# An mLSTM and mixture-of-experts kernel: SyncE's transfers in the recurrent part wait for the sixth one before them

## The chip, the cores and the metric

One core of a Trainium2 chip runs the whole program in one launch. The metric is the device time of an execution in microseconds, as the median of several executions.

## What is computed

The first part is an mLSTM layer on 4 batches x 8 heads, 768 steps, head size 40. Each step of the reference updates a matrix state and gives one row of the output:

```python
m_new = np.maximum(f_gate[:, :, t] + m, i_gate[:, :, t])
f_stab, i_stab = np.exp(f_gate[:, :, t] + m - m_new), np.exp(i_gate[:, :, t] - m_new)
C = f_stab[:, :, None, None] * C + i_stab[:, :, None, None] * np.einsum('bhd,bhe->bhde', vt, kt)
n = f_stab[:, :, None] * n + i_stab[:, :, None] * kt
h_tilde = np.einsum('bhde,bhe->bhd', C, qt)
denom = np.maximum(np.abs(np.einsum('bhd,bhd->bh', n, qt)[:, :, None]), 1.0)
y[:, :, t] = 1.0 / (1.0 + np.exp(-o_gate[:, :, t])) * h_tilde / denom
```

The second part takes the 3072 rows of that output (320 wide). It sends each to the one of 8 experts whose embedding is closest, and that expert gives `relu(x @ w1) @ w2` (1024 hidden units), times the router's share.

## The kernel before

The mLSTM is computed in tiles of 128 steps of one batch: 24 tiles, numbered `n`, in the order of the steps with the four batches inside. One turn of the Python loop `for n in range(NS)` is called a step below. The program is written out in full, and every engine's order of work is the order in which the source issues it (a manual schedule); waits are derived from the buffers.

In a step TensorE adds the tile's keys and values to the state (`stage_add`, L610), computes the scores of the next tile (`stage_scores`, L571), turns an earlier tile for the router (L716 to L718), sums the output (`stage_y`, L653 and L664) and scores it against the embeddings (L730). GpSimd scales the values of tile `n + 2` (`stage_uv`, L556) and multiplies the output of tile `n - 1` by its gate (`stage_gate`, L700). VectorE masks the scores (L580), divides (L696) and does the router's small operations. ScalarE copies.

All bulk transfers of this part are issued by SyncE, one after the other, in this order in each step `n`:

- `load_dims(n + 5)`: two loads into `kq_s` (L541), each of 40 rows of 4096 bytes (160 KB). There are NQ = 6 buffers, so the buffer of tile `n - 1` must be free.
- `load_rows(n + 5)`: one load into `kv_s` (L537), 128 rows of 2592 bytes (324 KB), also 6 buffers.
- `stage_sig(n + 3)`: one load of the output gate into `sig` (L550), 160 KB.
- `stage_store(n - 1)`: one store of the gated rows to `x_d` in DRAM (L704), 160 KB, which waits for L700.
- From step 9 on, in the steps of `W_AT`, one piece of an expert's weights into `raw` (L173 to L179), 256 to 512 KB.

Before the loop, the loads of tiles 0 to 4 and of the first gates are issued in the same way. After step 23 come the experts: first hidden products of the earliest tokens (L374), sums (L406), then the six other experts with weights that arrive one expert ahead. Transfers of that part are issued by SyncE (weights, and stores `x_d<-halves` followed by transposes at L1470) and by GpSimd (gathers and scatters).

Nothing in the source before limits how many of SyncE's transfers are under way.

Of the kernel before, what the change touches and what calls it, by code (L numbers as in the profile page):

```python
# [26 lines left out]
DM = H * D  # L27
P = 128
L = 64
# [4 lines left out]
NQ = 6  # L34
# [24 lines left out]
EMB_AT = (2, 3, 4)  # L59
ROOTS = {6: (0, 4), 10: (4, 8), 15: (8, 13), 18: (13, 16), 22: (16, 20)}  # L60
FILLS = (9, 3, 3)
NK = 2
NJ = NW // NK
RANGE = 60.0
# [5 lines left out]
def tile_mlstm_moe(  # L70
# [22 lines left out]
    V, G, A, T, SY = nc.vector, nc.gpsimd, nc.scalar, nc.tensor, nc.sync  # L93
# [65 lines left out]
    wrev_p = cp.tile([P, E], F32, name="wrev_p")  # L159


    def load_expert(e, at=None):
        raws, ws = {}, {}
        w1_, w2_ = (w[e] if at is None else w[ds(at, 1)].rearrange("o p f -> (o p) f") for w in (w1, w2))

        def load(i, part=None):
            def go():
                if not part:
                    raws[i] = wp.tile([P, F], F32, name=f"raw_{e}_{i}", tag="raw", bufs=7)
                raw = raws[i]  # L170
                w = slice(0, F) if part is None else slice(part * (F // 2), (part + 1) * (F // 2))
                if i < 2:
                    SY.dma_start(raw[:, w], w1_[i * P : (i + 1) * P, w])  # L173
                elif i == 2:
                    SY.dma_start(raw[0:L, w], w1_[2 * P : DM, w])
                    SY.dma_start(raw[L:P, w], w1_[2 * P : DM, w])
                else:
                    c = slice(2 * (i - 3), 2 * (i - 3) + 2)
                    SY.dma_start(  # L179
                        raw[:, 0 : 2 * DM].rearrange("p (c d) -> p c d", c=2),  # L180
                        w2_.rearrange("(c p) d -> p c d", p=P)[:, c],
                    )

            return go

        def piece(i, half, eng=None, on_act=True):
            def go():
                if i < 3:
                    c = slice(half * 512, half * 512 + 512)
                    h, lo, src = ws["w1h"][:, i, c], ws["w1l"][:, i, c], raws[i][:, c]  # L190
                else:
                    c = 2 * (i - 3) + half
                    h, lo, src = ws["w2h"][:, c], ws["w2l"][:, c], raws[i][:, half * DM : (half + 1) * DM]
                if on_act:
                    A.copy(h, src)  # L195
                else:
                    V.tensor_copy(h, src)
                (eng or V).tensor_tensor(lo, src, h.bitcast(F32), ALU.subtract)  # L198

            return go  # L200

        def tiles(pool, k):
            for t in "hl":
                shape = [P, 3, F] if k == 1 else [P, FC, DM]
                ws[f"w{k}{t}"] = pool.tile(shape, F32R, name=f"w{k}{t}_{e}", tag=f"w{k}{t}")

        return dict(ws=ws, tiles=tiles, load=load, piece=piece)
# [270 lines left out]
    with ExitStack() as actx:  # L478
# [20 lines left out]
        en = wp.tile([E, DM], F32, name="en", tag="raw", bufs=7)  # L499
# [13 lines left out]
        kv_s = [ap1.tile([P, KV], F32, name=f"kv_s{i}") for i in range(NQ)]  # L513
# [10 lines left out]
        st, sigs, xs_, grp = {}, {}, {}, {}  # L524
# [9 lines left out]
            return (t[:, a : a + 2 * NP * d].rearrange("p (c a d) -> p c a d", c=2, a=NP) for a, d in ((0, D), (m, D1)))  # L534

        def load_rows(n):
            SY.dma_start(kv_s[n % NQ], kv[n])  # L537

        def load_dims(n):
            for r in range(2):  # L540
                SY.dma_start(  # L541
                    kq_s[n % NQ][r * L : r * L + D, r : r + 2].rearrange("d w a t -> d (w a t)"),
                    kq[n, r].rearrange("d w a t -> d (w a t)"),
                )

        def stage_sig(n):
            j, b = divmod(n, B)
            if b == 0:
                sigs[j] = tp.tile([P, B, DM], F32, name=f"sig_{j}", tag="sig", bufs=2)
            SY.dma_start(sigs[j][:, b], og[:, n])  # L550

        def stage_uv(n, engs=None):
            j, b = divmod(n, B)
# [147 lines left out]

        def stage_store(n):
            j, b = divmod(n, B)
            SY.dma_start(xrows(j)[:, b, 0:DM], xs_[j][:, b])  # L704


        def stage_sq(n):
# [30 lines left out]
        def xrows(j):  # L738
            return x_d[0:NT].rearrange("(j b p) d -> j p b d", b=B, p=P)[j]
# [276 lines left out]
        V.memset(naught, 0.0)  # L1016
        fill(FILLS[0])
        V.memset(flat(kq_s[1]), 0.0)
# [13 lines left out]
        for n in range(3, 5):  # L1032
            load_dims(n)
            load_rows(n)
            if n == 3:
                SY.dma_start(en, emb)
        stage_sig(2)
        A.dma_start(taub, tau.partition_broadcast(P))

# [160 lines left out]
        w_loads, exps = [], {}  # L1200
# [9 lines left out]
        for n in range(NS):  # L1210
            last = n == NS - 1
            if n + 5 < NS:
                load_dims(n + 5)
                load_rows(n + 5)
            if n + 3 < NS:
                stage_sig(n + 3)
            if n == W_AT[0]:
                for k in range(NE):
                    exps[k] = load_expert(
                        k, nc.values_load(first[0:1, k : k + 1], engines=[ET.SP], min_val=0, max_val=E - 1)  # L1220
                    )
                exps[0]["tiles"](wp, 1)
                w_loads = [exps[0]["load"](i, part) for part in range(2) for i in range(3)]
                w_loads += [exps[0]["load"](i) for i in range(3, 7)] + [exps[1]["load"](i) for i in range(2)]
            stage_add(n, 0)
            stage_mid(n)
            for k in of(n - 1, 1, NEXT_AT):
                stage_keep(k)
            if n == 1:
                gates_exp()  # L1230
                A.activation(maxc.bitcast(F32), half, AF.Sigmoid)
            if n == 2:
                stage_sigmoid(1)
            if not last:
                stage_scores(n + 1)
            if n + 2 < NS and n not in (1, 2):
                stage_uv(n + 2)
            if n == NS - 4:
                gates_early[2]()
            if n:  # L1240
                for k in range(3):
                    stage_den(n - 1, k)
                stage_x(n - 1)
                for k in of(n, 1):
                    stage_gate(k, G if n < NS - 2 else V)
            if n == 1:
                stage_uv(n + 2)
            if n == NS - 3:
                for i in range(NE * HT):
                    gather_a(*divmod(i, HT))  # L1250
            if not last:
                stage_weigh(n + 1)
            for k in of(n, 1, NEXT_AT):
                stage_next(k)
            route(n)
            tick(9)
            if n == 0:
                gates_floor()
            if n == 1:
                gates_spread()  # L1260
            if n == 2:
                gates_turn()
                stage_uv(n + 2)
            if n == EMB_AT[2]:
                embeddings(2)
            if last:
                x_tile(xa[0], xs_a[:, 0], 0, pS, "ps")
            for k in of(n, 2):
                stage_xt(k)
            if last:  # L1270
                x_tile(xa[0], xs_a[:, 0], 1, pM, "pm")
            stage_y(n)
            if n < NS - B:
                stage_add(n, 1)
            if n != 1:
                stage_sigmoid(n)
            if n == 0:
                A.activation(maxc.bitcast(F32), half, AF.Exp)
            for k in of(n, 1):
                stage_store(k)  # L1280
            for k in of(n, 2):
                stage_sq(k)
            if n in EMB_AT[:2]:
                embeddings(EMB_AT.index(n))
            if n == 3:
                numbers()
            if n in (5, 6):
                G.memset(xs_a[:, n - 5], 0.0)
            if n == 5:
                more_numbers()  # L1290
            for k in of(n, 3, (EMB_AT[2],)):
                stage_logits(k)
            for _ in range(W_AT.count(n)):
                if w_loads:
                    w_loads.pop(0)()
            if n in W1_AT:
                exps[0]["piece"](*PIECES1[W1_AT.index(n)], G)()
            if n in ROOTS:
                gates_root(*ROOTS[n])
# [51 lines left out]
        n, g = NS - 1, len(GROUPS) - 1  # L1351
# [171 lines left out]
    for i in range(NE * HT):  # L1523
        e, a = divmod(i, HT)
# [14 lines left out]
    for e in range(NE, E):  # L1539
        j = e - NE  # L1540
        ws, x, w = exps[e]["ws"], xp, slice(0, CAPS[j])
        xps, turns, gt = [], [], gts[j]
        if e + 1 < E:
# [7 lines left out]
            n = CAPS[j + 1]  # L1551
# [30 lines left out]
    with tc.If(over > 0):  # L1582
        with ExitStack() as octx:
# [15 lines left out]
            with tc.For_i(0, steps, 1) as t:  # L1599
# [12 lines left out]
                kv = op.tile([NH, D, D], F32, name="kv")  # L1612
# [19 lines left out]
            with tc.For_i(0, again, 1):  # L1632
                V.tensor_copy(expert, num)
                for n in range(NS):
                    j, b = divmod(n, B)
# [46 lines left out]
            with tc.For_i(0, E, 1) as k:  # L1682
# [10 lines left out]
                with tc.For_i(0, NS, 1) as t:  # L1693
                    xo = op.tile([P, XW], F32, name="xo")
                    go = xo[:, DM:XC]
# [9 lines left out]
                    for c in range(3):  # L1705
                        w = min(P, DM - c * P)
# [3 lines left out]
                    for f in range(FC):  # L1710
                        ph = pv.tile([P, 512], F32, name=f"ovh_{f}", tag="ovh")
                        for c in range(3):
                            w = min(P, DM - c * P)
# [71 lines left out]
```

## Time and profile before

| what | value |
|---|---|
| time, median of 3 executions | 324.54 us (321.11 to 327.33) |
| profiled execution, its own time | 324.12 us |
| its span, first to last instruction | 322.3 us |
| TensorE busy | 299.6 us (93%) |
| VectorE, ScalarE, GpSimd busy | 217.6, 167.2, 169.6 us |
| SyncE's data queue, share of 16 DMA engines' time | 57.5% |

The profiled execution took 1.8 us more than its span. The mLSTM's steps fill the span from about 10 to 112 us, the experts the rest. A page of the profile cuts the span in 40 slices of 8.06 us; its first 14 digits belong to the mLSTM. "Issue" in a list of waits or in the chain is time in which an engine waited for nothing that the profile shows.

### The profile page before, as it was taken

Reading aid. Unit: us, or ns where it says so; the run is one execution under the profiler, and the core shown is the slowest. Engines: PE = TensorE matmul, PEld = TensorE weight load, DVE = VectorE, ACT = ScalarE, POOL = GpSimd, SP = SyncE. Lnnn points to the kernel's source line nnn. Section 1 sums busy time; section 2 is a strip of 40 time slices with the busy share of each in tenths; the row PEclk is TensorE's granted clock in tenths of the full one; section 3 lists DMA queues with packets and bytes.
Section 4 is the critical chain, followed back from the end, with each engine's and each line's share of the span. In section 5 each row is a group of like instructions: output and inputs, shape, how many; then the busy total and the mean of one; then the engine's idle time right before and its main releaser. Section 6 shows DMA issues by size and latency. Waiting matters only on the chain.

```text
span 322.3 us, 9598 instructions
## 1 busy us (share of the span) xinstructions
PE 299.6 (93%) x3637; PEld 284.5 (88%) x3637; DVE 217.6 (68%) x607; ACT 167.2 (52%) x429; POOL 169.6 (53%) x205
## 2 busy tenths in 40 slices
PE   6899996998777999999879999999999999999992
PEld 2889996997676999899879999999999999999992
DVE  7777896858894579865544876666756696586630
ACT  6676774775643586253232754546337266265310
POOL 8788865787867178150752850640650751632112
PEclk9799999999989799999979999999999999999998
DMA  5898998999986682130479968968948929837001
GB/s 136 261 303 295 287 278 266 263 272 290 284 238 174 183 222 71 13 86 2 125 243 181 301 189 210 320 195 235 247 150 228 290 94 288 235 103 219 21 22 39
DMA packets 48089, 63.31 MB, mean 196 GB/s; under 512 B 21146, under 2 KB 37990, under 8 KB 48034
## 3 DMA queue, kind: packets, MB, share of 16 engines
q1 hardware_dynamic: 45218, 54.16, 57.5%
q0 software_dynamic: 2560, 8.35, 8.9%
q8 instruction: 31, 0.51, 0.7%
q14 instruction: 24, 0.20, 0.2%
q10 hardware_dynamic: 256, 0.10, 0.1%
HBM read 47.51 MB, written 11.93 MB: 184 GB/s over the span
## 4 chain that ended last, share of the span: by engine, by line
PE 77%; DVE 11%; ACT 4%; issue 3%; DMA 3%; another core or an unknown queue 0%; POOL 0%; POOLq 0%; DVEq 0%; ACTq 0%; SPq 0%
PE ph L374 27%; PE po L406 17%; PE s L571 7%; PE y L653 4%; PE po_b L406 4%; PE y L664 3%; PE c L610 3%; PE po L391 3%; DMA kq_s<-in_kq 2%; PE pm L730 2%; PE po_a L406 2%; PE px L716 1%; ACT w2h L195 1%; DMA x_d<-x 1%; DVE w_s L580 1%
## 5 line engine op out<-in xcount | busy, mean ns | idle before, releaser
L425 POOL DMA_INDIRECT out<-ob,ids x20 | 22.2, 1112 | 75.4 <-DVE ob L422 64.6
L376 ACT ACTIVATE hh<-ph 128x448 fp32r<-128x448 f32 (+2 forms) x48 | 23.6, 492 | 42.8 <-PE ph L374 23.7
L406 PE MATMUL po<-w2h,hl 128*128 128x320 f32 x128 | 39.6, 309 | 0.0
L406 PE MATMUL po<-w2h,hh 128*128 128x320 f32 x128 | 39.5, 309 | 0.0
L406 PE MATMUL po<-w2l,hh 128*128 128x320 f32 x128 | 39.5, 309 | 0.0
L556 POOL TENSOR_TENSOR uv<-kv_s,u_t 64x328 f32<-64x328 f32 x47 | 35.0, 744 | 5.8 <-DMA kv_s<-in_kv 3.1
L571 PE MATMUL s<-kq_s 128*64 128x64 f32 x768 | 30.5, 230 | 4.6 <-issue 3.8
L571 PEld LDWEIGHTS s<-kq_s 128*64 128x64 f32 x768 | 27.8, 144 | 6.1 <-issue 4.5
L379 DVE SCALAR_TENSOR_TENSOR hl<-ph,hh 128x384 fp32r<-128x384 f32 (+1 forms) x48 | 24.4, 509 | 12.4 <-ACT hh L376 11.6
L374 PE MATMUL ph<-xh,w1h 128*128 128x448 f32 (+2 forms) x96 | 32.0, 336 | 0.0
L374 PE MATMUL ph<-xh,w1l 128*128 128x448 f32 (+2 forms) x96 | 32.0, 336 | 0.0
L195 ACT CAST w1h<-raw 128x512 fp32r<-128x512 f32 x48 | 28.9, 613 | 2.2 <-DMA raw<-in_w 2.2
L195 ACT CAST w2h<-raw 128x320 fp32r<-128x320 f32 x62 | 24.6, 457 | 7.0 <-DMA raw<-in_w 5.2
L422 DVE TENSOR_SCALAR ob<-po,gt 128x320 f32<-128x320 f32 x16 | 8.8, 550 | 27.9 <-PE po L406 19.8
L198 DVE TENSOR_TENSOR w2l<-raw,w2h 128x320 fp32r<-128x320 f32 x58 | 26.5, 504 | 1.1 <-ACT w2h L195 0.5
L297 POOL DMA_INDIRECT xs<-x_d,ids x20 | 22.9, 1143 | 6.2 <-issue 5.8
L198 DVE TENSOR_TENSOR w1l<-raw,w1h 128x512 fp32r<-128x512 f32 x36 | 24.7, 694 | 1.5 <-ACT w1h L195 1.5
L653 PE MATMUL y<-uv,w_s 128*64 128x82 f32 x384 | 24.8, 249 | 0.0
L374 PE MATMUL ph<-xl,w1h 128*128 128x448 f32 (+2 forms) x96 | 24.5, 336 | 0.0
L626 ACT COPY c_mid<-c 40x164 f32<-40x164 f32 x48 | 14.0, 292 | 19.7 <-PE c L610 15.6
L406 PEld LDWEIGHTS po<-w2l,hh 128*128 128x128 f32 x128 | 24.0, 188 | 0.0
L406 PEld LDWEIGHTS po<-w2h,hh 128*128 128x128 f32 x128 | 24.0, 188 | 0.0
(313 smaller groups left out, 912.8 us busy)
## 6 DMA issues: line engine op xcount, KB each, us to landing
raw<-in_w SPq DMA_DIRECT2D x32, 320.0 KB
kv_s<-in_kv SPq DMA_DIRECT2D x24, 324.0 KB
kq_s<-in_kq SPq DMA_DIRECT2D x48, 160.0 KB
raw<-in_w SPq DMA_DIRECT2D x14, 512.0 KB
raw<-in_w SPq DMA_DIRECT2D x18, 256.0 KB
sig<-in_og SPq DMA_DIRECT2D x24, 160.0 KB
x_d<-x SPq DMA_DIRECT2D x24, 160.0 KB
x_d<-halves SPq DMA_DIRECT2D x4, 576.0 KB
```

The costliest lines, as they stand in the source:

```text
L195: A.copy(h, src)
L198: (eng or V).tensor_tensor(lo, src, h.bitcast(F32), ALU.subtract)
L297: G.indirect_dma_start(out=xs[0 : c.shape[0], a], out_offset=None, in_=x_d[0:rows], in_offset=bass.IndirectOffsetOnAxis(ap=c, axis=0), bou ...
L374: T.matmul(ph, lt, rh, start=i == 0, stop=i == len(ops) - 1)
L376: A.activation(hh, ph, AF.Relu)
L379: V.scalar_tensor_tensor(hl[:, 0:m], ph[:, 0:m], 0.0, hh[:, 0:m].bitcast(F32), ALU.max, ALU.subtract)
L406: T.matmul(po[0 : ts_.stop - ts_.start, 0:DM], lt[f][:, ts_], rh[:, f], start=k == 0, stop=k == len(ops) - 1)
L425: store = G.indirect_dma_start(out=out, out_offset=bass.IndirectOffsetOnAxis(ap=slots, axis=0), in_=ob, in_offset=None, bounds_check=NT - ...
L556: eng.tensor_tensor(uv[n % NB][rows, :, :, r], list(rows_of(n))[1][rows], u_t[rows, j, b].unsqueeze(3).broadcast_to([L, 2, NP, D1]), ALU.mult,
L571: T.matmul(s[r * L : r * L + L, c, p], k_of(n, odd)[:, a, cs], q_of(n)[:, a, cs], start=True, stop=True,)
L626: A.copy(dst, src)
L653: T.matmul(yh[c][:, g, :, odd], w_s[n % NB][:, c, 2 * g + odd], uv[n % NB][:, c, 2 * g + odd], start=g + odd == 0, stop=n < B and c == 0, ...
```

## The change

Each of the transfers named above goes through a new function `paced`, which keeps a list in the order of issue. From the seventh on, a transfer gets a dependency on the one six places ahead of it: SyncE issues it only when that one has landed. Not in the list are the first gates (L507), the row of zeros (L1192), the gates' columns (L472), the weights that are issued after the loop, and everything of the experts' part.

```diff
+UNDER_WAY = 6
+    under_way = []
+    def paced(dma):
+        under_way.append(dma.ins)
+        if len(under_way) > UNDER_WAY:
+            tc.add_manual_dep(
+                dma.ins,
+                under_way[-1 - UNDER_WAY].name,
+                mybir.DependencyInfo(mybir.DependencyClass.Sync, mybir.DependencyReason.DATA),
+                reason="few transfers under way",
+            )
...
-            def go():
+            def go(send=SY.dma_start):
...
-                    SY.dma_start(raw[:, w], w1_[i * P : (i + 1) * P, w])
+                    send(raw[:, w], w1_[i * P : (i + 1) * P, w])
...
-            SY.dma_start(kv_s[n % NQ], kv[n])
+            paced(SY.dma_start(kv_s[n % NQ], kv[n]))
...
-                SY.dma_start(
+                paced(SY.dma_start(
                     kq_s[n % NQ][r * L : r * L + D, r : r + 2].rearrange("d w a t -> d (w a t)"),
...
-            SY.dma_start(sigs[j][:, b], og[:, n])
+            paced(SY.dma_start(sigs[j][:, b], og[:, n]))
...
-            SY.dma_start(xrows(j)[:, b, 0:DM], xs_[j][:, b])
+            paced(SY.dma_start(xrows(j)[:, b, 0:DM], xs_[j][:, b]))
...
-                SY.dma_start(en, emb)
+                paced(SY.dma_start(en, emb))
...
-                    w_loads.pop(0)()
+                    w_loads.pop(0)(lambda *a: paced(SY.dma_start(*a)))
```

## Rows read from the trace of the kernel before

**Rows 1.** The page: busy tenths in 40 slices, and a DMA queue (packets, MB, share).

```profile
PE   6899996998777999999879999999999999999992
DMA  5898998999986682130479968968948929837001
...
q8 instruction: 31, 0.51, 0.7%
```

**Rows 2.** Timeline of SyncE's queue, 1 to 16 us: start, duration, line, transfer.

```profile
1.94 0.68 SPq L541 DMA_DIRECT2D kq_s<-in_kq  x2
2.66 0.36 SPq L537 DMA_DIRECT2D kv_s<-in_kv  x1
3.70 0.66 SPq L541 DMA_DIRECT2D kq_s<-in_kq  x2
4.40 0.40 SPq L537 DMA_DIRECT2D kv_s<-in_kv  x1
4.84 0.50 SPq L550 DMA_DIRECT2D sig<-in_og  x1
6.35 0.69 SPq L541 DMA_DIRECT2D kq_s<-in_kq  x2
7.52 0.35 SPq L537 DMA_DIRECT2D kv_s<-in_kv  x1
```

**Rows 3.** Timeline of TensorE, 5 to 40 us; in brackets idle time and what ended it.

```profile
7.64 1.15 PE L571 MATMUL s<-kq_s 128*64 128x64 f32 x32 [0.56 <-DMA kq_s<-in_kq]
...
10.54 1.97 PE L571 MATMUL s<-kq_s 128*64 128x64 f32 x32 [0.15 <-DMA kq_s<-in_kq]
```

**Rows 4.** The chain that ended last, in order of time: start, duration, work.

```profile
36.45 0.93 PE s L571 x32
...
40.07 0.93 PE s L571 x32
...
43.35 0.31 PE c L610 x8
```

**Rows 5.** Timeline of GpSimd, 5 to 52 us.

```profile
14.55 1.54 POOL L556 TENSOR_TENSOR uv<-kv_s,u_t 64x328 f32<-64x328 f32 x2 [0.68 <-DMA kv_s<-in_kv]
...
36.49 1.58 POOL L556 TENSOR_TENSOR uv<-kv_s,u_t 64x328 f32<-64x328 f32 x2
```

**Rows 6.** Stretches: busy us of PE, PEld, DVE, ACT, POOL; clock, DMA share, GB/s.

```profile
20.00:24.00 4.00, 4.00 (x95) 3.76 (x94) 2.75 (x13) 3.15 (x12) 3.20 (x5) 1.00 0.91 311
44.00:48.00 4.00, 4.00 (x111) 3.71 (x107) 3.67 (x14) 2.84 (x11) 2.46 (x5) 1.00 0.92 281
52.00:56.00 4.00, 1.57 (x31) 1.15 (x28) 2.24 (x7) 1.16 (x4) 1.36 (x2) 1.00 0.79 246
84.00:88.00 4.00, 2.18 (x62) 1.98 (x57) 3.44 (x11) 1.28 (x6) 3.85 (x5) 1.00 0.90 277
...
94.50:98.30 3.80, 3.80 (x74) 3.77 (x70) 2.47 (x10) 1.99 (x8) 3.13 (x4) 0.55 0.64 142
```

**Rows 7.** SyncE's waits, whole span: us in total, times, longest.

```profile
SPq L1470 <- DMA x_d<-halves: 11.0, 6, 2.6
...
SPq L541 <- DMA kq_s<-in_kq: 5.2, 10, 0.9
SPq L550 <- DMA kq_s<-in_kq: 5.2, 10, 0.9
```

**Rows 8.** Timeline of TensorE at its two longest "issue" waits.

```profile
55.00 0.33 PE L718 MATMUL px<-ident,x 128*128 128x128 f32 x1 [2.43 <-issue]
...
87.13 0.69 PE L571 MATMUL s<-kq_s 128*64 128x64 f32 x17 [1.82 <-issue]
```

**Rows 9.** Timeline of SyncE's queue, 47 to 89 us.

```profile
47.12 0.70 SPq L541 DMA_DIRECT2D kq_s<-in_kq  x2
...
54.64 0.35 SPq L550 DMA_DIRECT2D sig<-in_og  x1
...
81.67 0.35 SPq L537 DMA_DIRECT2D kv_s<-in_kv  x1
...
88.50 0.53 SPq L175 DMA_DIRECT2D raw<-in_w  x1
```

More of the change, by code (lines that the diff above doesn't have):

```diff
@@ L172, in go @@
                 if i < 2:
-                    SY.dma_start(raw[:, w], w1_[i * P : (i + 1) * P, w])
+                    send(raw[:, w], w1_[i * P : (i + 1) * P, w])
                 elif i == 2:
-                    SY.dma_start(raw[0:L, w], w1_[2 * P : DM, w])
-                    SY.dma_start(raw[L:P, w], w1_[2 * P : DM, w])
+                    send(raw[0:L, w], w1_[2 * P : DM, w])
+                    send(raw[L:P, w], w1_[2 * P : DM, w])
                 else:
                     c = slice(2 * (i - 3), 2 * (i - 3) + 2)
-                    SY.dma_start(
+                    send(
                         raw[:, 0 : 2 * DM].rearrange("p (c d) -> p c d", c=2),
@@ L536, in load_rows @@
         def load_rows(n):
-            SY.dma_start(kv_s[n % NQ], kv[n])
+            paced(SY.dma_start(kv_s[n % NQ], kv[n]))
         def load_dims(n):
             for r in range(2):
-                SY.dma_start(
+                paced(SY.dma_start(
                     kq_s[n % NQ][r * L : r * L + D, r : r + 2].rearrange("d w a t -> d (w a t)"),
                     kq[n, r].rearrange("d w a t -> d (w a t)"),
-                )
+                ))
         def stage_sig(n):
```

## The prediction

> **What bounds the kernel now.** I read the page first, for where TensorE and the DMA engines are both full; then the timeline of SyncE's queue, because the change touches nothing else; then the timelines of TensorE and GpSimd for who starts at the moment a transfer lands; and the stretches for the price of a step.
>
> TensorE is nearly full for most of the span [rows 1]. In the mLSTM from 20 to 52 us it is full: 4.00 of 4.00 us in the stretches at 20 and 44 us [rows 6], and the scores of one tile follow those of the last after 40.07 - 36.45 = 3.62 us [rows 4]. In the same stretches the 16 DMA engines are busy 0.91 and 0.92 of the time [rows 6]. So this part runs on two resources of about the same length; TensorE ends last.
>
> Before about 17 us it is the transfers that end last. TensorE's scores of tiles 0 and 1 start at 7.64 and 10.54 us, each on a `kq_s` transfer [rows 3], and GpSimd's scaling of tile 2 at 14.55 us on a `kv_s` transfer [rows 5].
>
> SyncE already holds transfers back. It waits ten times for a `kq_s` transfer before it issues another `kq_s`, and ten times before a `sig` [rows 7], though those transfers share no buffer. How far back that reaches can be counted in the list of issues [rows 2]: the load of tile 2's `kv_s` goes out at 7.52 us, next to TensorE's start at 7.64 us on tile 0's second `kq_s` transfer [rows 3]. Between that transfer (issued at about 2.3 us) and the `kv_s` load stand `kv_s` 0, two `kq_s` 1, `kv_s` 1, `sig` 0 and two `kq_s` 2, which are seven; so the one eight places ahead was awaited. **So the kernel has at most eight under way, and the change makes it six**, not six in place of any number.
>
> **Does a transfer land later?** A step issues 5 transfers (two `kq_s`, `kv_s`, `sig`, the store) in 3.62 us, one in 0.72 us. With eight under way, each may take 8 x 0.72 = 5.8 us from issue to landing. By the count above it is 5.3 us at the start (2.3 to 7.6). With six, each may take 6 x 0.72 = 4.3 us. The question is what of the 5.8 us is the transfer's own and what is queue. A lone transfer shows the first: SyncE waits for the landing of the stores `x_d<-halves` 11.0 / 6 = 1.8 us after their issue [rows 7], with an issue of about 0.4 us (`kv_s` at 4.40 us, rows 2) 2.2 us in all. So 3.6 us are queue, and a DMA share of 0.9 [rows 6] says the same: the engines have work waiting. With six, a new transfer finds five ahead of it, 5 x 0.72 = 3.6 us of work, and needs at most 2.2 us to take its place behind them. The engines don't run dry; cover 1.4 us. Transfers go out later by up to 1.5 us and land as before. Cost: 0.
>
> Behind a waiting transfer on SyncE stand the next loads, the gate loads and the stores. Who waits for them: TensorE for `kq_s`, GpSimd for `kv_s`. If the cover of 1.4 us is gone, a second one stands behind it in the steps: GpSimd scales tile 9 at 36.49 us, is done at 38.07 us [rows 5], and TensorE adds the product at 43.35 us [rows 4], 5.3 us later. At the start there is none: tile 2's scaling ends at 16.09 us [rows 5], about when TensorE needs it. What the start could lose is bounded by 0 and, if the latency of 5.3 us stayed with six under way, by 2.0 us: nine transfers stand ahead of `kv_s` 2, and 5.3 / 6 = 0.88 us for each in place of 5.3 / 8 = 0.66 makes 2.0 us. I take 0, for the queue argument holds there too.
>
> Stores land in DRAM for gathers much later. Pieces of weights stand among paced transfers in steps 9 to 23; each waits for the sixth before it in place of the eighth, 1.5 us later, and lands behind the same queue: 0. The wait itself costs no engine but SyncE, which computes nothing. The experts' part is not touched: 0.
>
> **What may be gained.** TensorE stops twice for nothing that the profile shows, 2.43 us before 55.00 us and 1.82 us before 87.13 us [rows 8]. These are the stretches in which its busy time falls to 1.57 and 2.18 of 4 us [rows 6]. A queue of its own brings 31 blocks of instructions, 0.51 MB [rows 1], and runs on the same 16 engines. The two stops fall where data is slowest: the second `kq_s` transfer of the row at 47.12 us has `sig` at 54.64 us as its eighth follower, 7.2 us later, and `kv_s` at 81.67 us has the weights at 88.50 us, 6.8 us later [rows 9], against the usual 5.8. If a block of instructions waits as data does, the queue ahead of it shrinks by 5.8 - 4.3 = 1.5 us, and so does each stop: at most 2.9 us. If it doesn't, 0. Nothing in the trace separates the two; I take the middle, 1.45 us. What is gained at 55 us reaches the end: TensorE is full after it.
>
> The Trainium skill, DMA: Bandwidth & Descriptors, section on queues, rings and completion order, says that a DMA engine takes turns between its queues, packet by packet. By that rule a block of instructions would never wait behind SyncE's whole queue, the stops would stay, and the time would be that of the second rival. No row here shows the order inside an engine.
>
> **The sum.** The profiled execution took 324.12 us, 322.3 of span and 1.8 around it. Landing later 0, gain 1.45: 322.7. The median of the runs stands 0.4 above the profiled one (324.54), so 323.1 us.
>
> **The rivals.**
>
> *Slower: the latency doesn't shrink.* If what I call queue is the transfer's own time under load, six under way give 6 in 5.3 us in place of 8: a step's five take 4.4 us, 0.8 more than TensorE's 3.62. Tiles 7 to 23 are loaded in steps 2 to 18, some 16 steps: 12.8 us, less the cover of 5.3 us, gives +7.5 us, 332 us. It decides from 0.33 us more in a step (5.3 / 16), that is from a landing time of 6 x (3.95 / 5) = 4.7 us with six under way. Against it: lone transfers at 2.2 us and a DMA share of 0.9. For it: TensorE and the DMA are so close to each other that little must go wrong.
>
> *No difference.* Transfers go out later and land as before, and the stops stay (or lie elsewhere): 324.5 us. For it: the stops may come from the moment of the request and not from its queue.
>
> *Faster: the stops go altogether.* 2.43 + 1.82 = 4.25 us, and with the second the slow clock may go: in the stretch at 94.5 us, 6.5 us behind the half-busy one at 84, the granted clock is 0.55 over 3.80 us (mostly the lower level, 1.2 GHz), 1.7 us lost [rows 6]. 324.5 - 5.95 = 318.6 us.
>
> **How the numbers follow.** Chances: the forecast 0.56, no difference 0.22, slower 0.12, faster 0.10. A measurement of this kernel can tell about 2%, 6.5 us: its three times lie 6.2 us apart. The forecast's own range is 321 to 326 (gain of 0 to 2.9, and half of the spread of the runs). To hold 8 in 10, the range reaches to 318.5, the faster rival, and to 329.5, a slower rival at two thirds of its price. Faster by over 2% (under 318) needs more than the faster rival's sum, 0.06; slower (over 331) is most of the slower rival, 0.09; within it 0.85.
>
> **What would show it.** In SyncE's timeline the first `sig` load moves from 4.84 to about 6.3 us and tile 2's first `kq_s` from 6.35 to about 7.5 us; counted six places back, a landing takes some 4.3 us. TensorE still starts scores at 7.6 and 10.5 us, and GpSimd tile 2 at about 14.6 us. The steps stay at 3.62 us with a DMA share of 0.9. The stops near 55 and 87 us shorten by about 1.5 us or not at all. Steps over 3.95 us, a DMA share near 0.75, and TensorE waiting for `kq_s` or for L556 after 20 us would make the slower rival right; times of scores before 17 us that are later by 1 us or more would show the start's cover gone.

## The result and the profile after

The changed kernel takes 328.75 us (median of 20 executions, 324.63 to 335.54), the kernel before beside it 324.25 us (20 executions, 320.44 to 327.33). The ratio of the two is 1.0112, 95% interval 1.0071 to 1.0153: **1.1% slower**, where 0.4% faster was forecast. The ratio is smaller than that of the medians because it leaves out disturbed executions, as do all ratios below. The profiled execution took 328.64 us, 326.9 of it span, against 324.12 and 322.3.

First what came as forecast. SyncE's timeline of the changed kernel (start, duration, line; lines behind the new function stand 14 higher than before, and the pieces of weights are now issued at L1309), which answers to [rows 2]:

```profile
2.66 0.37 SPq L551 DMA_DIRECT2D kv_s<-in_kv  x1
...
6.27 0.35 SPq L564 DMA_DIRECT2D sig<-in_og  x1
7.58 1.14 SPq L555 DMA_DIRECT2D kq_s<-in_kq  x2
9.49 0.35 SPq L551 DMA_DIRECT2D kv_s<-in_kv  x1
```

`sig` has moved from 4.84 to 6.27 us and tile 2's `kq_s` from 6.35 to 7.58 (forecast: 6.3 and 7.5). The first users start when they did, TensorE's scores of tiles 0 and 1 [rows 3] and GpSimd's scaling of tile 2 [rows 5]:

```profile
7.66 1.72 PE L585 MATMUL s<-kq_s 128*64 128x64 f32 x32 [0.58 <-DMA kq_s<-in_kq]
...
10.60 1.51 PE L585 MATMUL s<-kq_s 128*64 128x64 f32 x32 [0.23 <-DMA kq_s<-in_kq]
```

```profile
14.54 1.56 POOL L570 TENSOR_TENSOR uv<-kv_s,u_t 64x328 f32<-64x328 f32 x2 [0.61 <-DMA kv_s<-in_kv]
```

Then what didn't. The same stretches as in [rows 6], with two more (columns as there: busy time of five engines, granted clock, DMA share, GB/s):

```profile
20.00:24.00 4.00, 4.00 (x98) 3.76 (x95) 2.82 (x13) 2.75 (x10) 2.76 (x5) 1.00 0.88 287
44.00:48.00 4.00, 3.89 (x105) 3.51 (x103) 3.70 (x12) 2.58 (x9) 2.79 (x4) 1.00 0.89 261
52.00:56.00 4.00, 3.79 (x107) 3.49 (x104) 3.90 (x10) 2.15 (x7) 3.85 (x5) 1.00 0.82 258
57.50:60.50 3.00, 0.09 (x3) 0.07 (x4) 2.23 (x7) 1.20 (x4) 0.54 (x1) 0.78 0.89 246
59.20:66.00 6.80, 5.57 (x84) 5.45 (x85) 1.82 (x8) 4.15 (x13) 5.73 (x7) 0.50 0.96 292
84.00:88.00 4.00, 4.00 (x114) 3.76 (x109) 2.98 (x8) 3.86 (x13) 2.35 (x3) 1.00 0.95 282
```

The stretches at 52 and 84 us, which TensorE's two stops had half emptied, are full: 3.79 and 4.00 us in place of 1.57 and 2.18. The stops of [rows 8] are gone altogether. But from 20 to 48 us the transfers move less: 311 GB/s at 20 us has become 287, 281 at 44 us 261. And a new hole stands at 57.5 us, where TensorE works 0.09 of 3.00 us, with the lower clock (0.50) for 6.80 us behind it.

The chain that ended last says what this is. By engine, over the whole span, before and then after:

```profile
PE 77%; DVE 11%; ACT 4%; issue 3%; DMA 3%; another core or an unknown queue 0%; POOL 0%; POOLq 0%; DVEq 0%; ACTq 0%; SPq 0%
```

```profile
PE 61%; DMA 23%; DVE 5%; POOL 3%; issue 3%; ACT 1%; another core or an unknown queue 1%; SPq 1%; POOLq 0%; DVEq 0%
```

Transfers make up 23% of the chain in place of 3%. Its pieces in the first 56 us (start, duration, what):

```profile
1.94 4.27 DMA kq_s<-in_kq
6.27 5.37 DMA sig<-in_og
11.65 5.10 DMA kq_s<-in_kq
16.77 4.11 DMA sig<-in_og
20.89 5.26 DMA kq_s<-in_kq
26.22 4.48 DMA kv_s<-in_kv
...
40.97 4.63 DMA kv_s<-in_kv
45.61 4.89 DMA sig<-in_og
...
55.75 3.49 DMA raw<-in_w
```

The first six pieces hang together, each beginning where the last one landed: 1.94 + 4.27 = 6.21, and the sixth follower goes out at 6.27. This is the change's own dependency, end to end, up to 30.70 us. After that the chain runs through GpSimd, TensorE and ScalarE as well, and only the piece at 45.61 us begins at a landing again. The trace's semaphore updates tell when every transfer has landed: 88 of the 111 paced transfers up to `kv_s` 23 go out within 0.15 us of the landing of the one six places ahead, the others later, for other reasons.

The lag of this list decides when the first piece of weights (`raw`) goes out, at 55.75 us. SyncE's lines around it, the kernel before and then the changed one:

```profile
49.02 0.35 SPq L550 DMA_DIRECT2D sig<-in_og  x1
...
51.46 0.36 SPq L173 DMA_DIRECT2D raw<-in_w  x1
```

```profile
49.46 0.35 SPq L551 DMA_DIRECT2D kv_s<-in_kv  x1
...
53.31 0.35 SPq L564 DMA_DIRECT2D sig<-in_og  x1
...
55.75 0.36 SPq L1309 DMA_DIRECT2D raw<-in_w  x1
```

The gate load `sig` at 53.31 us waits for the `kv_s` load six places ahead, which was issued at 49.46 and landed at 53.25 us. From this gate load to the piece 2.44 us pass in both kernels.

That piece ends the hole at 57.5 us. ScalarE's cast of it, of the kernel before and then of the changed one, with TensorE's stop:

```profile
57.18 0.62 ACT L195 CAST w1h<-raw 128x512 fp32r<-128x512 f32 x1 [0.52 <-DMA raw<-in_w]
```

```profile
59.26 0.62 ACT L209 CAST w1h<-raw 128x512 fp32r<-128x512 f32 x1 [4.62 <-DMA raw<-in_w]
59.79 0.59 ACT L640 COPY c_mid<-c 40x164 f32<-40x164 f32 x2
...
60.43 0.40 PE L678 MATMUL y<-c_mid,kq_s 128*64 128x82 f32 x1 [2.91 <-ACT c_mid L640]
```

The piece goes out 4.29 us later. ScalarE stands 4.62 us for it, and behind the cast in ScalarE's order stands the copy `c_mid`, which TensorE's sum needs: 2.91 us. The lower clock from 59.2 us begins within that stop. The cast starts 2.08 us later than before, for the late piece landed sooner after its issue (3.49 us). By this count the other 0.8 us of the stop would have been left with the piece on time: without its first stop TensorE reaches this place about 2 us sooner.

Where the time went, by the starts of TensorE's scores (us):

| what starts | before | after | difference |
|---|---|---|---|
| scores of tile 12 | 51.10 | 51.45 | +0.4 |
| tile 13 (first stop of before lies ahead of it) | 57.35 | 55.33 | -2.0 |
| tile 14 | 60.95 | 63.55 | +2.6 |
| tile 16 | 68.29 | 72.13 | +3.8 |
| tile 21 (second stop of before lies ahead of it) | 90.31 | 92.49 | +2.2 |
| tile 23 | 100.62 | 103.70 | +3.1 |
| first hidden product of the experts | 111.52 | 114.60 | +3.1 |
| end of span | 322.3 | 326.9 | +4.6 |

The first stop gone gives 2.4 us. From tile 13 to 16, 5.9 us are lost: the stop of 2.91, and the lower clock over 5.57 us of TensorE's work, half of which (2.8) is its price at a granted clock of 0.50. The second stop gone gives 1.7 back. The last 1.5 us are lost in the experts' part, where the lower clock lasts 6.8 us from 165.0 in place of 3.4 us from 162.9; the change paces no transfer there, and what lengthens the low clock isn't shown.

### The profile page after: what moved, and what is told of

Same layout as the page of the kernel before. It is cut to its first block, busy times and chain, and to the rows that moved or that the text cites. A ratio compares the mean times of both kernels' runs of the same rounds, so it can differ in the third digit from the quotient of the medians.

```text
span 326.9 us, 9598 instructions
## 1 busy us (share of the span) xinstructions
PE 302.7 (93%) x3637; PEld 287.3 (88%) x3637; DVE 218.6 (67%) x607; ACT 167.3 (51%) x429; POOL 170.0 (52%) x205
## 4 chain that ended last, share of the span: by engine, by line
PE 61%; DMA 23%; DVE 5%; POOL 3%; issue 3%; ACT 1%; another core or an unknown queue 1%; SPq 1%; POOLq 0%; DVEq 0%
PE ph L388 27%; PE po L420 17%; DMA kq_s<-in_kq 9%; DMA sig<-in_og 6%; PE po_b L420 4%; PE po L405 3%; DMA kv_s<-in_kv 3%; DMA raw<-in_w 2%; PE s L585 2%; DMA xs_a<-x_d,ids_a 2%; PE y L667 2%; PE y L678 2%; PE c L624 1%; POOL uv L570 1%
## 5 line engine op out<-in xcount | busy, mean ns | idle before, releaser
L585 PE MATMUL s<-kq_s 128*64 128x64 f32 x768 | 29.2, 231 | 1.0 <-DMA kq_s<-in_kq 1.0
L212 DVE TENSOR_TENSOR w2l<-raw,w2h 128x320 fp32r<-128x320 f32 x58 | 27.2, 515 | 0.6
L678 PE MATMUL y<-c_mid,kq_s 128*64 128x82 f32 x192 | 23.1, 246 | 3.0 <-ACT c_mid L640 2.9
L311 POOL DMA_INDIRECT xs<-x_d,ids x20 | 21.5, 1073 | 6.2 <-issue 5.8
```

The source lines that it names most:

```text
L311: G.indirect_dma_start(out=xs[0 : c.shape[0], a], out_offset=None, in_=x_d[0:rows], in_offset=bass.IndirectOffsetOnAxis(ap=c, axis=0), bou ...
L585: T.matmul(s[r * L : r * L + L, c, p], k_of(n, odd)[:, a, cs], q_of(n)[:, a, cs], start=True, stop=True,)
L678: T.matmul(yh[c][:, g, r], q_of(n)[:, 2 * g + r, c * L : c * L + L], state[:, 2 * g + r].rearrange("p (s d) -> p s d", s=2), start=False, ...
```

## The experiments

Theory: with fewer under way the transfers go slower, SyncE's list falls behind, and some user of a late transfer stops TensorE. Rivals: one late piece of weights is all; the pace of the list has nothing to do with it; what is lost belongs to one series of runs. A number used for all: the time from SyncE's issue of `kv_s` 5 to that of `kv_s` 10, divided by the 25 transfers between (22 where gate loads are merged). Ratios are against the kernel before in the same series of runs.

### Only one late piece of weights?

`e1_six_cast12` (the changed kernel) and `e2_before_cast12` (the kernel before) cast the first piece a step later:

```diff
-W1_AT = (11, 13, 15, 17, 19, 21)
+W1_AT = (12, 13, 15, 17, 19, 21)
```

> Six under way as in the changed kernel, but the first cast of a piece of weights stands in step 12 in place of step 11. Theory A (late weights): with six under way SyncE falls 4.3 us behind by step 9, the first piece is issued at 55.75 us in place of 51.46, ScalarE stands 4.62 us before its cast, TensorE stops 2.91 us for c_mid behind it and then has the low clock for 6.8 us. Then this kernel has none of the three and takes about 323 us (5 to 6 less than the changed kernel's 328.75). Theory B (rate only): the cast isn't special, some other wait for the later transfers takes its place: 327 to 329 us.

> The kernel before with the same move of the first cast to step 12, no pacing. Theory A: the wait there was 0.52 us and hidden, so nothing changes: 324 us, ratio 0.997 to 1.003. Theory C: the move itself gains, pacing or not: 4 us or more less than before.

Measured: e1 330.03 us, ratio 1.0138 (1.0072 to 1.0203); e2 325.72, 1.0012 (0.9965 to 1.0058). In e1 the hole near 58 us and its low clock are gone, and tile 23 starts at 99.9 us, 0.7 before the kernel before. Yet the time is lost again. Lines of e1's timelines of SyncE, GpSimd and TensorE, and a stretch:

```profile
99.96 0.43 SPq L486 DMA_DIRECT2D x_d<-sw  x1
...
105.55 1.31 POOL L311 DMA_INDIRECT xs_a<-x_d,ids_a  x1 [5.52 <-DMA x_d<-sw]
...
112.04 0.88 PE L366 MATMUL pa<-ident,xs_a 128*128 128x128 f32 x3 [8.62 <-DMA xs_a<-x_d,ids_a]
```

```profile
107.50:117.50 10.00, 5.46 (x54) 4.82 (x55) 2.03 (x8) 2.67 (x8) 5.02 (x6) 0.50 0.86 292
```

`x_d<-sw` writes the router's columns behind the rows; it isn't paced, but it stands at the end of SyncE's list. It goes out at 99.96 us (before: 92.55), the gather waits 5.52 us for it, TensorE 8.62 us for the gather, and 10 us of low clock follow. The rival falls: with the first late user out of the way, the next one takes over.

### How the pace goes with the number under way

`e3_seven` and `e4_four`: `UNDER_WAY = 7` and `= 4` in place of 6.

> Seven under way in place of six. Theory A: SyncE falls behind by about half as much by step 9, the first piece lands about 2 us later than before, ScalarE stands 1 to 3 us: 325 to 327 us. Theory B gives the same order but in proportion to the transfers' rate: 326.5 us. If seven already equals six, 328.7, the cost doesn't come from the number under way but from the order in which waits are placed.

> Four under way. By the argument of the prediction (a lone transfer takes 2.2 us, the rest is queue) four still come to 4 / 2.9 = 1.4 transfers a us, and the time is that of six: 328 us. By what the changed kernel showed (landing after 4.5 us, at 1.33 transfers a us) four land after some 3.3 us, which is 1.2 a us or 4.1 us for a step: loads fall behind by 0.5 us in each of 16 steps, past what is hidden, and every step after the eighth waits: 333 to 340 us.

Measured: seven 324.69 us, ratio 1.0000 (0.9956 to 1.0044); four 348.7, 1.0698 (1.0603 to 1.0792). Both lie outside what was expected, seven below it (325 to 327 us) and four above it (333 to 340). SyncE's issues of `kv_s` 5 and 10 with eight (before), seven, six (the changed kernel) and four under way:

```profile
17.30 0.35 SPq L537 DMA_DIRECT2D kv_s<-in_kv  x1
...
33.62 0.35 SPq L537 DMA_DIRECT2D kv_s<-in_kv  x1
```

```profile
18.24 0.35 SPq L551 DMA_DIRECT2D kv_s<-in_kv  x1
...
35.81 0.35 SPq L551 DMA_DIRECT2D kv_s<-in_kv  x1
```

```profile
18.68 0.35 SPq L551 DMA_DIRECT2D kv_s<-in_kv  x1
...
37.08 0.35 SPq L551 DMA_DIRECT2D kv_s<-in_kv  x1
```

```profile
21.95 0.35 SPq L551 DMA_DIRECT2D kv_s<-in_kv  x1
...
44.78 1.02 SPq L551 DMA_DIRECT2D kv_s<-in_kv  x1
```

| under way | us for 25 transfers | each | times the number: issue to landing | mean landing by the semaphore updates |
|---|---|---|---|---|
| 8 | 16.32 | 0.653 | 5.2 | 5.2 |
| 7 | 17.57 | 0.703 | 4.9 | 4.8 |
| 6 | 18.40 | 0.736 | 4.4 | 4.3 |
| 4 | 22.83 | 0.913 | 3.7 | 3.8 |

From four to eight the landing time grows by (5.22 - 3.65) / 4 = 0.39 us for each further transfer under way; drawn back to none, an estimate of 2.1 us is left. In these four traces the pace rises with every transfer added, up to eight, and a transfer takes 13% longer with six than with eight. The number isn't all: `g3_before_cast12_put` below has eight under way and needs 18.00 us, 0.720 each, where the other kernels with eight need 0.653 to 0.663; seven need 0.703 and 0.706, six 0.736 to 0.774. TensorE's 3.62 us a step ask for a transfer every 0.724 us. Seven stay just below that and six just above it, which fits that seven cost nothing.

In e4 the stretches 16 to 30 and 30 to 50 us show engines that stand idle for a quarter to 30% of the time:

```profile
16.00:30.00 14.00, 11.17 (x245) 9.84 (x245) 8.50 (x29) 8.19 (x27) 9.16 (x20) 1.00 0.75 217
30.00:50.00 20.00, 18.85 (x469) 17.75 (x467) 13.28 (x50) 12.00 (x39) 12.46 (x19) 0.92 0.70 203
```

### The second late user moved off SyncE's list

The put of the router's columns issued by ScalarE: `g4_six_put` alone, `g1_six_cast12_put`, `g2_seven_cast12_put` (seven under way) and `g3_before_cast12_put` (the kernel before) with the later cast.

```diff
-            SY.dma_start(x_d[n0 * P : n1 * P, DM:XW]..., sw)
+            (SY if n0 else A).dma_start(x_d[n0 * P : n1 * P, DM:XW]..., sw)
```

> Six under way, first cast in step 12, and the store of the first gates' columns (L486, in step 20) issued by ScalarE in place of SyncE. Theory D (the end of SyncE's list): SyncE's list is what ends last; in the run with the cast in step 12 the columns were ready at 92.8 us, went out at 99.96 behind two gate loads, a store and weights, the gather waited 5.5 us and TensorE stood 8.62 us before the gathered rows and had the low clock for 10 us. With the store out of SyncE's list the gather starts at about 101 us, the stand falls to 2 us or less: 321 to 324 us, that is 5 to 8 less than the 330.0 of that run. Theory B (rate only, everywhere): the gain is under 2 us, since the next thing in SyncE's list (loads for tiles 22 and 23) takes over.

> Seven under way with both moves. Theory D: seven was already the time of before (324.7); its stop of 1.5 us for c_mid behind the late cast and part of its 3.6 us before the gathered rows go: 320 to 323 us. Theory B: 324.5.

> No pacing, both moves: the control. The columns were issued 1.6 us after they were ready, and TensorE's stops of 2.4 to 2.8 and 1.2 to 1.8 us at block boundaries of its instructions stay: 323 to 325 us, ratio 0.99 to 1.00. If it gains as much as the paced kernels do, the moves have nothing to do with pacing.

> The changed kernel with only the store of the columns moved to ScalarE. Theory A with D: the late cast in step 11 still costs 2.9 us and the low clock for 6.8 us, so the list's end was hidden behind it in part: 326 to 328 us, 1 to 3 less than the changed kernel.

| kernel | us | ratio (95%) | put goes out | gather starts |
|---|---|---|---|---|
| g1, six | 329.45 | 1.0204 (1.0116 to 1.0293) | 99.74 | 104.5 |
| g2, seven | 324.48 | 1.0047 (0.9992 to 1.0102) | 94.98 | 101.4 |
| g3, before | 326.8 | 1.0078 (1.0017 to 1.0140) | 95.59 | 100.7 |
| g4, six, early cast | 328.87 | 1.0184 (1.0104 to 1.0264) | 98.69 | 106.5 |

A miss as a remedy: on ScalarE the put is as late as on SyncE. ScalarE's timeline in g1 shows it standing for it, from 93.5 to 99.7 us, though the columns were done at 92.2:

```profile
92.89 0.60 ACT L653 COPY c_st<-c 40x164 f32<-40x164 f32 x2
99.74 0.43 ACTq L486 DMA_DIRECT2D x_d<-sw  x1
```

SyncE's next transfer in that kernel goes out at 99.68 us, in the same moment. The trace tells why: the transfers of SyncE and ScalarE use eight semaphores in turn, and the put waits for the one of SyncE's `sig` load of 94.76 us, eight places ahead in both engines' common order, which landed at 99.66 us. ScalarE's stand then stops TensorE for 1.54 us (before 100.84 us), so the move has a cost of its own; g3, without pacing, comes to 1.0078 where 0.99 to 1.00 was expected, and its put goes out later than that of the kernel before (92.55 us). The runs tell less than planned about the second place. They do repeat the order: seven 0.5%, not clear of nothing, six 1.8 to 2.0%.

### Only early, or only late

`h3_six_to9_cast12` paces until step 8 alone (with the later cast), `h4_six_from10` from step 10 on. The lines of h4 (h3 begins with True and sets False at `n == 9`):

```diff
-        if len(under_way) > UNDER_WAY:
+        if len(under_way) > UNDER_WAY and pacing[0]:
...
+            if n == 10:
+                pacing[0] = True
```

> Six under way only until step 8, no pacing from step 9 on, and the first weights cast in step 12. Rate theory: the lag of some 3 us at step 9 is made up or held at eight's rate, ScalarE's cast finds its weights, the put before the experts is on time within 2 us of before: 322 to 325.5 us. Rival (what six does early is lost for good): 327 us and over.

> Pacing by six only from step 10 on. Rate theory: the first weights piece is on time, so no stop of TensorE at the c_mid of step 11 and no low clock near 59 us; the list then falls behind by 0.3 us a step over some 12 steps, so the put goes out 2 to 4 us later than before and TensorE stands longer before the first pa: 325 to 328 us. Rival (the whole loss is the stop near 58 us): 322 to 324.5 us.

The kernel before took 318.5 us in this series (23 executions), some 2% less than earlier, so the expected times are to be read as ratios to it. h3: 321.1 us, 1.0070 (1.0024 to 1.0116); h4: 321.68 us, 1.0131 (1.0078 to 1.0185). Of h3 the theory had expected at most 1.004: **it was wrong in that the lag would be made up.** Step `n` loads tile `n + 5`, so its transfers go unpaced from `kv_s` 14 on. There SyncE is 4.3 us behind the kernel before (52.38 against 48.04), at `kv_s` 18 3.0 us (70.04 against 67.00) and at `kv_s` 23 again 4.8 us (89.92 against 85.17), though eight may be under way. A part is made up and lost again; why the 27 transfers from `kv_s` 18 to 23 take 19.88 us in place of 18.17 isn't shown. h4 costs a little more than the 1.002 to 1.011 expected. No stop near 58 us, and TensorE waits 1.98 and 0.97 us for the gather; the put goes out at 96.64 us. Either half of the pacing is enough to lose.

### Fewer transfers, the same bytes

If the number under way sets the pace, fewer and larger transfers must win it back. The gate loads of four tiles as one transfer of the same bytes (4.25 transfers a step in place of 5; the first four gate loads stay single): `h1_six_sig4` at six, `h2_before_sig4` in the kernel before.

```diff
-            paced(SY.dma_start(sigs[j][:, b], og[:, n]))
+            if j == 0:
+                paced(SY.dma_start(sigs[j][:, b], og[:, n]))
+            elif b == 0:
+                paced(SY.dma_start(sigs[j], og[:, n : n + B]))
```

> Six under way, as in the changed kernel, but the gate loads of four tiles go out as one transfer of the same bytes, so that SyncE has 4.25 transfers a step in place of 5. Rate theory (a transfer takes about 1.9 us that passes whatever the number under way, and 0.46 us for each one under way, fitted to the list's pace at eight, seven, six and four): the merged bytes make the work per transfer 0.53 us, the latency 5.1 us, and a step of the list 4.25 x 5.1 / 6 = 3.6 us, about what seven under way gave (3.93 less the weights' share); most of the loss goes: 324 to 326.5 us, and SyncE's kv loads of steps 5 to 23 go out within about 71 us. Rival (the loss has nothing to do with the number of transfers on the list): 328 to 329.5 us, kv issues spread over 73 us as in the changed kernel.

> The same merged gate loads in the kernel before (eight under way). Rate theory: the list goes faster than TensorE needs it (about 3.3 us a step against 3.6), so the time hardly moves: 322 to 325 us, ratio 0.99 to 1.00. Rival (the instruction blocks wait behind the queued data): more bytes under way lengthen TensorE's two issue stops, 324 to 326 us with the stops at 2.4 us or over.

h1: 319.69 us, ratio 1.0025 (0.9981 to 1.0069), in the series in which h3 and h4 lost. h2: 320.48 us, 1.0104 (1.0044 to 1.0163), slower, against the theory's 0.99 to 1.00. That series held no run of six itself, so a last one put the kernel before, six, six merged and seven merged side by side:

> The kernel before, unchanged, for its profile beside the other three on one chip at one time: ratio 1.00. Its SyncE list between the kv loads of steps 5 and 10 goes at 3.2 to 3.4 us a step, the put before the experts goes out by 93 to 95 us.

> The changed kernel, unchanged, beside the others. Rate theory (SyncE's list gets late with six under way): ratio 1.008 to 1.016, list at 3.65 to 3.8 us a step between steps 5 and 10, the put at 97 us or later. Rival (the loss belongs to some chips or times only): ratio 0.995 to 1.005.

> Six under way with the gate loads of four tiles in one transfer, 4.25 transfers a step. Rate theory: list at 3.45 to 3.6 us a step, the put near 96 us, and a ratio at least 0.006 below that of six alone, 0.998 to 1.006. Rival (the merged loads win nothing back): the same ratio as six alone within 0.004.

> Seven under way with the merged gate loads. Rate theory: list at about 3.3 us a step between steps 5 and 10, as before, and TensorE's issue stops shorter than at eight: ratio 0.994 to 1.002. Rival (the merged loads themselves cost 1%, as they seemed to at eight): 1.005 to 1.012.

| kernel | us | ratio (95%) | a step of the list, `kv_s` 5 to 10 | put goes out |
|---|---|---|---|---|
| k1, before | 318.35 | 0.9997 (0.9955 to 1.0039) | 3.27 us | 91.81 |
| k2, six | 327.41 | 1.0253 (1.0185 to 1.0320) | 3.76 | 100.68 |
| k3, six, merged | 320.39 | 1.0079 (1.0033 to 1.0125) | 3.50 | 94.84 |
| k4, seven, merged | 318.94 | 1.0003 (0.9954 to 1.0051) | 3.23 | 92.56 |

k2 has six executions, the other three twelve each. The same bytes and the same six under way: merging one load in five wins back 1.0253 - 1.0079 = 1.7 points, two thirds of the loss. It also puts more bytes into the same six places, so the runs don't tell the number under way from the bytes under way. The steps of the list came out as expected (3.45 to 3.6 us for k3, about 3.3 for k4), the ratios of k2 and k3 higher (1.008 to 1.016 and 0.998 to 1.006 expected). The loss lies in the paced part: the experts' first hidden product starts at 117.47 us in k2 and at 108.13 in k1, 9.3 us apart, and the spans end 9.5 us apart. TensorE's stop for `c_mid`, 2.91 us in the changed kernel and 3.90 in k2, is down to this in k3:

```profile
60.51 0.28 PE L681 MATMUL y<-c_mid,kq_s 128*64 128x82 f32 x1 [1.26 <-ACT c_mid L643]
```

And k4 shows that the merge costs nothing by itself where seven are under way. Why it cost 1.0% at eight (h2) stays open. h2's list is no faster than that of the kernel before (3.23 us a step), and the lower clock stands for 3.4 us behind a stop of 2.01 us near 55 us (and for 3.4 us more from 91.1 us); k4 has a stop of 2.48 us at the same place and no low clock.

No version was faster than the kernel before by more than its interval.

## Why the prediction was wrong

**What bounds the kernel: right, and not heeded.** TensorE and the DMA engines were called two resources of about the same length. Then a slower pace of one of them (13% more time for a transfer) was priced at nothing.

**Eight under way, not any number: right.** Seven costs nothing, six costs 1.1 to 2.5% and four 7%; the first issues came out within 0.1 us of their forecast places. The traces show the eight themselves, as the eight semaphores that these transfers use in turn.

**"The engines don't run dry; cover 1.4 us": the step that failed.** The landing time did fall with the number, from 5.2 to 4.4 us (4.3 forecast, and 4.3 by the semaphore updates), so the slower rival's mechanism (it stays) was wrong as well. But the argument took the queue as an all-or-nothing matter: 5 x 0.72 = 3.6 us of work ahead against 2.2 us, so the engines are always fed. The runs show a pace that rises with the number under way, 1.10 per us with four, 1.36 with six, 1.42 with seven, 1.53 with eight (1.39 in g3). By the estimate above one more transfer ahead adds 0.39 us to a landing, not 0.72; five add 2.0 us, which is less than the 2.2 us they were to cover. By this the cover was none. The 0.72 us was the interval at which TensorE wanted the transfers, and was used as the work of one. The 2.2 us was read too low: the waits of [rows 7] count from SyncE's last instruction, which in four of the six cases is a second store. Where a store stands alone in the kernel before (214.05 and 239.38 us), the transpose that waits for it goes out 3.05 and 3.09 us after it (217.10 and 242.47).

Why the engines stand idle with five transfers queued isn't shown. Unevenly spread work on 16 engines would do it, and a `kq_s` load of 40 rows raises its semaphore in 11 updates where a load of 128 rows takes 16, but no view here tells the engines apart.

By the Trainium skill, DMA: Bandwidth & Descriptors, section Anatomy of one DMA — SWDGE (gpsimd) path, a transfer issued by GpSimd has a fixed part of about 2.0 us. The 2.1 us drawn back from these runs of SyncE's transfers lies close to it, but no run here measures that part alone.

**"Pieces of weights ... lands behind the same queue: 0": failed with it.** Each piece was to wait 1.5 us longer and land as before; a slower pace isn't a shift of 1.5 us. The list's lag adds up over steps: 1.4 us at `kv_s` 5, 3.5 at `kv_s` 10, 6.7 at `kv_s` 23 (91.88 against 85.17). The first piece went out 4.29 us late and landed 2.1 us late, and the cover was not looked up: in the trace before, ScalarE's cast already waits 0.52 us for that piece, so it had none. The cover that was worked out, 5.3 us from GpSimd's scaling to TensorE's use, held: TensorE has no wait of over 0.4 us for a `kv_s` product in the changed kernel's steps.

**The start: right.** The scores of tiles 0 and 1 and the scaling of tile 2 start within 0.1 us of before; loss 0.

**The gain in TensorE's stops: right in kind, under-sized.** 1.45 us was taken, 2.9 as the most. In the changed kernel both stops are gone, 4.25 us. Added up between 45 and 95 us (stops over 0.4 us), eight under way has 4.25, 4.01, 4.36 and 3.74 us (before, e2, g3, k1), seven 0.97 and 1.65 (e3, g2), six 0, 0.63, 0, 1.30 and 0.57 (the changed kernel, e1, g1, g4, k2), four none. With merged gate loads it is 4.93 us at eight (h2), 2.48 at seven (k4), 1.61 and 0.54 at six (h1, k3); with pacing in a part of the steps 1.67 and 1.46 (h3, h4). So the stops do shrink with the number of transfers under way, each kernel by its one trace. What they are can be read from the packets of the instruction queue: every such stop between 40 and 95 us, in all kernels, ends 1.3 to 1.6 us behind the end of a packet of 16384 bytes (in the kernel before 55.00 behind 53.53, and 87.13 behind 85.66 us). TensorE waits for its next block of instructions. In the changed kernel the block of the first stop moves from 49.62 us in place of 52.32, though TensorE's tile 12 starts 0.4 us later. From 46 to 52 us the DMA queues' view has no packet of the instruction queue q8 in the kernel before and one in the changed kernel.

That the stops would stay, which was drawn from the rule of turns between queues in the Trainium skill (DMA: Bandwidth & Descriptors, Queues, rings and completion order), is not borne out here; what the rule leaves out, no run shows.

**The sum.** Of the span's 4.6 us: 4.25 us of stops gained, 5.7 us lost to a new stop with its low clock, 0.9 at a wait for VectorE (2.79 us before 96.38 us, 1.87 before 93.28 earlier), 0.4 before tile 12 and 1.5 in the experts' clock. That is 8.5 us lost less 4.25 gained; 0.35 of the 4.6 stays unexplained. Seven gains part of the stops and loses little: even. The "faster" rival's 4.25 us came and were spent; its slow clock near 95 us didn't go, but stands from 96.8 to 100.2 us at 0.50.

The range held the time (328.75 of 318.5 to 329.5), because it had been stretched to the slower rival. As that rival's mechanism isn't what happened, this is luck. The chance of a loss was given only for one of over 2% (0.09); the measured one lies below that.

## What to carry to other kernels

In this kernel, with DMA engines 0.9 busy, the number of transfers under way was a resource. Count it in the list of issues, price taking some away as a slower pace over the whole list, not as a shift of each transfer, and compare that pace with the one that the busiest engine asks for (here 0.736 to 0.774 us with six against 0.724). A lag in one engine's list adds up until its first user without a margin meets it; look in the trace before for users that already wait for the last link of that list, however shortly (here 0.52 us). If fewer must be under way, larger ones may help, for the same bytes then need fewer places: it won back two thirds here, but cost 1.0% with eight under way.

## What was not expected of the hardware

- A low clock follows a stop and adds to its price: behind the stop of 2.91 us it costs another 2.8 us, as much again. In e1 a stop of 8.62 us from 103.4 us on goes with 10 us at a granted clock of 0.50 from 107.5, with 5.46 us of TensorE's work in them, half of which (2.7) is lost.
- The same kernel before took 324.3, 325.9, 326.3, 318.5 and 318.5 us in five series of runs (medians). The profile from the last one (k1) has a span of 316.8 us against 322.3, with the clock at 1.00 from 15.5 to 312.5 us; the three pieces at 0.50 near 95, 105 and 163 us aren't there. With such steps between series, only kernels of one series can be compared at 1%.
- A transfer moved from SyncE to ScalarE to leave SyncE's line waited there until SyncE's next one went out too (99.74 and 99.68 us), for both engines' transfers take turns on the same eight semaphores.
